# Fewer weight decodings beside the first eight head pairs, the rms weight folded into the decoding, and a new order for the first pair

## The chip, the cores and the metric

The kernel runs on one core of a Trainium2 chip. The metric is the time of one execution on the device, in microseconds (us), as a median of several runs. A measurement of this kernel tells differences of about 0.5% (6.7 us) from no change.

## The reference

```python
# q, k, v: 8 batches x 8 heads x 576 tokens x 64, w_phi: 64 x 128
proj = x @ w_phi;  proj = proj - max|proj| (per token)
phi(x) = [exp(proj), exp(-proj)]                 # 256 features
kv = sum_s phi(k) v;  z = sum_s phi(k)
attn = (phi(q) kv) / (phi(q) z + 1e-6)           # -> x: 4608 tokens x 512
xn = x / sqrt(mean(x*x) + 1e-6) * rms_g
g = xn @ w_gate;  val = xn @ w_val               # 512 x 1536 each
out = (silu(g) * val) @ w_out                    # 1536 x 512
```

The three weights and `rms_g` of the second half are stored as 64-bit floats (`rms_g` as read by the kernel is 32-bit); the kernel turns each weight into 32-bit floats itself, and calls that decoding. Products that have to be exact are computed from a high and a low part of each operand, as three matmuls (high x high, high x low, low x high).

## The kernel before, in words

The program has three stages: the attention (0 to about 525 us), the products with `w_gate` and `w_val` (to about 1065 us), and the product with `w_out`. The change touches the attention stage.

**Rounds.** The 64 heads are taken as 32 pairs. The loop at line 500 runs over rounds `i`. In round i, `front(i)` transposes and projects pair i, `mid(i-1)` takes exponentials and accumulates kv for the pair before, `back(i-2)` forms numerator and denominator, `last(i-3)` divides and stores the result to `xs` in DRAM. The inverse of the denominator goes through DRAM by four DMAs one after the other: `dd` out, `dr` in, reciprocal, `di` out, `rc` in as a broadcast (lines 419 to 428); line 442 then waits for `rc`.

**front.** `trans` transposes k (`kt`), q (`qt`) or the rests (`rb`, the 64 tokens of k and q that don't fill a block of 128) and splits the result into `th` and `tl` (line 61 on VectorE). `proj` multiplies by the split `w_phi` (`wh`, `wl`, lines 311 to 313), takes the largest magnitude (`mx`, line 315) and subtracts it (`yk`, `yq`, `yr`, line 318). There are two PSUM buffers `pp` and three `sm`.

**Decoding.** Each round takes one job from `decs` (`dq += 1`, line 510): one fetch of 128 x 384 weights (`raw`), two ScalarE instructions (lines 48, 49), three VectorE instructions on bits (50 to 52), two GpSimd products (54), and one VectorE sum (55). The first eight jobs belong to `wf1`, the part of the weights that stays in SBUF: there line 235 multiplies by `g`, the rms weight, and `_split` makes a high and a low part (lines 60, 61; `fg`, `fv`). The other 24 are written to DRAM (`wgs`, `wvs`).

**Fills.** From about 191 us the first products with `wf1` (line 474, `fp<-xo`) run beside the attention. A block of 288 tokens is fetched (`x<-xs`, line 142), split into `xo` (lines 60, 61), and gives six units. When the attention ends the remaining units run alone. `x0`, the first block of the second stage, is fetched in round 27 and its squares (lines 147, 150) are placed from round 29.

**Order.** The code gives pieces positions within a round (`_spread`, `_merge`), and a scheduler then fixes the order of instructions on each engine. On each engine, and in each DMA queue, instructions start in that order: one that waits holds all behind it. `late()` ties an instruction behind those already issued on its engine.

Of the kernel before, what the change touches and what calls it, by code (L numbers as in the profile page):

```python
# [8 lines left out]
F32 = mybir.dt.float32  # L9
F32R = mybir.dt.float32r  # L10
I32 = mybir.dt.int32
U32 = mybir.dt.uint32
AF = mybir.ActivationFunctionType
ALU = mybir.AluOpType
# [23 lines left out]
    return raw  # L38


def _decode(nc, pool, raw, n):
    if raw.dtype == F32:
        return raw
    low, high = raw[:, :, 0], raw[:, :, 1]
    p = pool.tile([128, n], I32, name="wp", bufs=2)
    a = pool.tile([128, n], F32, name="wa", bufs=2)
    u, lf = a.bitcast(I32), low.bitcast(F32)
    nc.scalar.mul(a, high.bitcast(F32), REBASE)
    nc.scalar.mul(lf, low.bitcast(U32), 2.0 ** -52)
    nc.vector.tensor_scalar(p, u, 3, None, ALU.logical_shift_left)  # L50
    nc.vector.scalar_tensor_tensor(p, u, -0x80000000, p, ALU.bitwise_and, ALU.bitwise_or)
    nc.vector.tensor_scalar(u, p, -0x00800000, None, ALU.bitwise_and)
    for h in (slice(0, n // 2), slice(n // 2, n)):
        nc.gpsimd.tensor_tensor(a[:, h], lf[:, h], a[:, h], ALU.mult)  # L54
    nc.vector.tensor_tensor(a, p.bitcast(F32), a, ALU.add)
    return a


def _split(nc, hi, lo, x, hi_copy=None, lo_eng=None):
    (hi_copy or nc.scalar.copy)(hi, x)  # L60
    (lo_eng or nc.vector).tensor_tensor(lo, x, hi.bitcast(F32), ALU.subtract)  # L61
# [21 lines left out]
def kernel(ctx: ExitStack, tc: tile.TileContext, q, k, v, w_phi,  # L83
                         w_gate, w_val, w_out, rms_g, out):
    nc = tc.nc
# [3 lines left out]
    NC, NJ = DM // 128, DF // 128  # L89
# [23 lines left out]
    gl = ctx.enter_context(tc.tile_pool(name="gl", bufs=1))  # L113
    eps = gl.tile([128, 1], F32, name="eps")
    nc.vector.memset(eps, 1e-6)
    g = gl.tile([128, NC], F32, name="g")

# [69 lines left out]
    dec = a_ctx.enter_context(tc.tile_pool(name="a_dec", bufs=1))  # L189
# [23 lines left out]

    vms = [const.tile([128, 2, T0, D + 1], F32, name=f"vm{i}") for i in range(3)]
    vrs = [const.tile([128, 2, D + 1], F32, name=f"vr{i}") for i in range(3)]
    for vm, vr in zip(vms, vrs):
        nc.gpsimd.memset(vm, 1.0)
        nc.gpsimd.memset(vr, 1.0)
        nc.gpsimd.memset(vr[64:128, 0], 0.0)
        nc.gpsimd.memset(vr[0:64, 1], 0.0)  # L220
# [8 lines left out]
    def decode_jobs():  # L229
        jobs, late_ = [], []  # L230
        n = J1 * 128
        for wi, src in enumerate((w_gate, w_val)):
            for c in range(NC):
                def fill_w(w, wi=wi, c=c):
                    nc.vector.tensor_scalar(w, w, g[:, c:c + 1], None, ALU.mult)
                    _split(nc, wf1[wi][0][:, c], wf1[wi][1][:, c], w)
                jobs.append((src[c * 128:(c + 1) * 128, 0:n], n, fill_w))

        def keep(jobs, src, dst, r0, c0, n):
            at = slice(r0, r0 + 128), slice(c0, c0 + n)  # L240
            jobs.append((src[at], n, lambda w: nc.sync.dma_start(out=dst[at], in_=w)))

        for c0 in range(n, DF, 384):
            for src, dst in ((w_gate, wgs), (w_val, wvs)):
                for c in range(NC):
                    keep(jobs, src, dst, c * 128, c0, 384)
        for j in range(NJ):
            for c0 in range(0, DM, CH):
                keep(late_, w_out, wos, j * 128, c0, CH)
        return jobs, late_  # L250

    def decode_pieces(jobs, dec):
        raws = {}

        def piece(i):
            if i == 0:
                raws[0] = _fetch(nc, dec, *jobs[0][:2])
            raw = raws.pop(i)
            if i + 1 < len(jobs):
                raws[i + 1] = _fetch(nc, dec, *jobs[i + 1][:2])  # L260
            with late():
                jobs[i][2](_decode(nc, dec, raw, jobs[i][1]))
        return [lambda i=i: piece(i) for i in range(len(jobs))]

    st = {}
# [20 lines left out]
    def front(pr):  # L286
        d = st[pr]
        f = {n: d[n].rearrange("p h t d -> p (h t d)") for n in ("kt", "qt")}
        us = {n: [f[n + "t"][:, i * 128:(i + 1) * 128] for i in range(4)] for n in "kq"}
        us["r"] = [d["rb"].rearrange("p a d -> p (a d)")]  # L290
        d["y"] = {}
        hl = {}

        def trans(n):
            m = len(us[n]) * 128
            tp = ps_s.tile([128, 512], F32, name="sm")
            for j, u in enumerate(us[n]):
                nc.tensor.transpose(out=tp[:, j * 128:(j + 1) * 128], in_=u, identity=ident)
            th = wk.tile([128, 512], F32R, name="th")
            tl = wk.tile([128, 512], F32R, name="tl")  # L300
            _split(nc, th[:, 0:m], tl[:, 0:m], tp[:, 0:m])
            hl[n] = (th, tl)

        def proj(n, u0):
            th, tl = hl[n]
            m = min(2, len(us[n]) - u0)
            pp = ps_p.tile([128, 4, F], F32, name="pp")
            for j in range(m):
                o = pp[:, 2 * j:2 * j + 2].rearrange("p a f -> p (a f)")
                cs = slice((u0 + j) * 128, (u0 + j + 1) * 128)  # L310
                nc.tensor.matmul(o, th[:, cs], wh, start=True, stop=False)  # L311
                nc.tensor.matmul(o, th[:, cs], wl, start=False, stop=False)
                nc.tensor.matmul(o, tl[:, cs], wh, start=False, stop=True)  # L313
            mx = wk.tile([128, 4], F32, name="mx")
            nc.vector.tensor_reduce(mx[:, 0:2 * m], pp[:, 0:2 * m], axis=AX.X, op=ALU.max,  # L315
                                    apply_absolute_value=True)
            y = wk.tile([128, 4 if n != "r" else 2, F], F32, name="y" + n, bufs=3 if n != "r" else 2)
            nc.vector.tensor_tensor(y[:, 0:2 * m], pp[:, 0:2 * m],  # L318
                                    mx[:, 0:2 * m].unsqueeze(2).broadcast_to([128, 2 * m, F]), ALU.subtract)
            d["y"][n, u0 // 2] = y  # L320

        return [lambda: trans("r" if pr else "k"), lambda: trans("k" if pr else "r"),
                lambda: proj("r", 0), lambda: proj("k", 0), lambda: trans("q"), lambda: proj("k", 2), lambda: proj("q", 0), lambda: proj("q", 2)]

# [161 lines left out]
    dq = quota = 0.0  # L486
# [8 lines left out]
            units.extend(fill(*here.pop(0)))  # L495

    load(0)
    nc.sync.dma_start(out=g, in_=rms_g.rearrange("(c p) -> p c", p=128))
    load(1)
    for i in range(PR + 3):  # L500
        streams = []
        if i < PR:
            streams.append(_spread(front(i), -0.2, 0.7))
# [3 lines left out]
            streams.append(back(i - 2))  # L507
        if 0 <= i - 3 < PR:
            streams.append(last(i - 3))
        dq += 1  # L510
        dl, decs = decs[:int(dq)], decs[int(dq):]
        dq -= int(dq)
        streams.append(dl)
# [30 lines left out]
    dec = g_ctx.enter_context(tc.tile_pool(name="m_dec", bufs=1, reuse_waits="tile"))  # L544
# [261 lines left out]
```

## Time and profile before

| | us |
|---|---|
| median of 3 runs | 1340.66 (1338.13 to 1345.27) |
| the profiled execution's own time | 1340.64 |
| its span, first to last instruction | 1338.7 |
| TensorE busy | 1288.7 (96%) |
| VectorE busy | 884.2 (66%) |
| ScalarE busy | 711.7 (53%) |
| GpSimd busy | 606.9 (45%) |

The busy shares are means over stages with different limits, and a matmul's duration overlaps its neighbours', so the number of matmuls in a stretch says more of TensorE than its busy time. PE is TensorE, DVE VectorE, ACT ScalarE, POOL GpSimd, SP the queue from which most DMAs are issued.

### The profile page before, as it was taken

The numbers are of one execution on the slowest core, as the hardware profiler recorded it, in microseconds if no ns is written. First come the engines' busy times: TensorE is split into PE (matmuls) and PEld (weight loads), VectorE is DVE, ScalarE is ACT, GpSimd is POOL, SyncE is SP. The second block draws the span as 40 slices with busy tenths as digits, with TensorE's granted clock in tenths as the row PEclk, the third lists the DMA queues.
The fourth block names the chain that finished last, engine by engine and source line by source line (L and its number), as shares of the span: only waits on it lengthen the run. The fifth ranks groups of instructions, "written<-read, shape, count | busy, mean of one in ns | idle before, by whom it ended". The sixth has DMA issues, their size and how long they took to land.

```text
span 1338.7 us, 25484 instructions
## 1 busy us (share of the span) xinstructions
PE 1288.7 (96%) x9396; PEld 1274.0 (95%) x9396; DVE 884.2 (66%) x1301; ACT 711.7 (53%) x1510; POOL 606.9 (45%) x568
## 2 busy tenths in 40 slices
PE   7989999999999897998999999999999999999998
PEld 6889899999999897998999999999999999999998
DVE  7899888787778772114566656655434498877774
ACT  5988877778778782344444344433333334434332
POOL 4766565555556570000232223233221078787675
PEclk9999999999999898999999999999999999999999
DMA  6456566665555434446454454554433533454451
GB/s 164 124 144 156 163 161 161 173 167 169 154 165 159 120 102 149 141 145 192 149 168 148 159 166 138 166 164 143 132 114 109 183 111 126 149 167 127 138 161 65
DMA packets 204524, 197.21 MB, mean 147 GB/s; under 512 B 69553, under 2 KB 186417, under 8 KB 204401
## 3 DMA queue, kind: packets, MB, share of 16 engines
q1 hardware_dynamic: 194896, 190.88, 47.9%
q10 hardware_dynamic: 9504, 4.72, 1.3%
q8 instruction: 74, 1.21, 0.4%
q14 instruction: 50, 0.40, 0.1%
HBM read 126.04 MB, written 69.50 MB: 146 GB/s over the span
## 4 chain that ended last, share of the span: by engine, by line
PE 55%; DVE 3%; DMA 2%; ACT 1%; issue 1%; POOL 0%; ACTq 0%; SPq 0%; DVEq 0%
PE fp L588 16%; PE gp L588 16%; PE fp L474 6%; PE gd L742 5%; PE gz L742 5%; PE gy L742 5%; PE fp L742 2%; DMA wc<-wvs 1%; DMA wc<-wgs 1%; DVE xo L61 0%; DVE a12l L61 0%; DMA rc<-di 0%; DVE a11l L61 0%; DVE ri L160 0%; POOL s2l L61 0%
## 5 line engine op out<-in xcount | busy, mean ns | idle before, releaser
L380 POOL TENSOR_TENSOR ql<-eq,qh 128x256 fp32r<-128x256 f32 x256 | 218.0, 882 | 66.2 <-issue 39.1
L588 PE MATMUL fp<-xb,wg 128*128 128x384 f32 x864 | 163.4, 337 | 4.4 <-ACT wg L60 4.3
L588 PE MATMUL gp<-xb,wv 128*128 128x384 f32 x864 | 161.5, 334 | 0.0
L588 PEld LDWEIGHTS fp<-xb,wg 128*128 128x128 f32 x864 | 152.1, 189 | 5.0 <-ACT wg L60 4.5
L588 PEld LDWEIGHTS gp<-xb,wv 128*128 128x128 f32 x864 | 150.9, 188 | 0.0
L573 DVE TENSOR_TENSOR h<-sl,gp 128x384 f32<-128x384 f32 x108 | 59.5, 551 | 127.6 <-PE gp L588 59.5
L571 ACT ACTIVATE sl<-fp 128x384 f32<-128x384 f32 x108 | 52.7, 489 | 165.8 <-PE fp L588 144.6
L54 POOL TENSOR_TENSOR wa<-raw,wa 128x192 f32<-128x192 f32 (+1 forms) x112 | 67.5, 623 | 159.6 <-ACT sl L571 51.7
L351 PE MATMUL acc<-vm,ek 128*128 128x65 f32 x1024 | 131.7, 271 | 0.0
L351 PEld LDWEIGHTS acc<-vm,ek 128*128 128x128 f32 x1024 | 128.1, 195 | 0.2 <-ACT ek L338 0.2
L315 DVE TENSOR_REDUCE mx<-pp 128x4 f32<-128x512 f32 (+1 forms) x160 | 100.4, 631 | 39.8 <-PE pp L313 38.2
L61 POOL TENSOR_TENSOR xb<-x,xb 128x1536 fp32r<-128x1536 f32 x12 | 42.8, 3563 | 151.7 <-ACT xb L60 151.7
L151 POOL TENSOR_TENSOR ss<-ss,sq 128x384 f32<-128x384 f32 x36 | 38.6, 1071 | 153.9 <-ACT sq L150 153.9
L474 PE MATMUL fp<-xo,fg 128*128 128x288 f32 x576 | 96.5, 305 | 9.1 <-DVE xo L61 9.1
L376 ACT ACTIVATE qh<-sm 128x512 fp32r<-128x512 f32 (+1 forms) x192 | 96.9, 505 | 0.0
L474 PEld LDWEIGHTS fp<-xo,fg 128*128 128x128 f32 x576 | 82.4, 191 | 12.4 <-DVE xo L61 11.4
L474 PE MATMUL fp<-xo,fv 128*128 128x288 f32 x576 | 92.5, 299 | 0.0
L311 PE MATMUL pp<-wh,th 128*128 128x256 f32 x288 | 88.2, 308 | 4.3 <-DVE yr L318 3.6
L61 POOL TENSOR_TENSOR s2l<-st,s2h 128x768 fp32r<-128x768 f32 x18 | 43.6, 2420 | 97.4 <-DVE h L573 44.2
L375 ACT ACTIVATE eq<-sm 128x512 f32<-128x512 f32 x128 | 78.1, 610 | 12.8 <-PE sm L364 11.7
L313 PE MATMUL pp<-wh,tl 128*128 128x256 f32 x288 | 82.3, 295 | 2.2 <-DVE tl L61 2.2
L588 PE MATMUL fp<-xb,fg 128*128 128x384 f32 x432 | 81.1, 335 | 0.6 <-ACT sl L571 0.5
(198 smaller groups left out, 3794.2 us busy)
## 6 DMA issues: line engine op xcount, KB each, us to landing
hs<-h SPq DMA_DIRECT2D x144, 192.0 KB
ht<-hs SPq DMA_DIRECT2D x18, 1536.0 KB
gvs<-fo SPq DMA_DIRECT2D x96, 144.0 KB
gvr<-gvs SPq DMA_DIRECT2D x36, 384.0 KB
rc<-di SPq DMA_DIRECT2D x32, 288.0 KB
x<-xs SPq DMA_DIRECT2D x16, 576.0 KB
x<-xs SPq DMA_DIRECT2D x12, 768.0 KB
kt<-in_k_dram SPq DMA_DIRECT2D x32, 256.0 KB
```

Of the source, the lines that this page charges most:

```text
L54: nc.gpsimd.tensor_tensor(a[:, h], lf[:, h], a[:, h], ALU.mult)
L61: (lo_eng or nc.vector).tensor_tensor(lo, x, hi.bitcast(F32), ALU.subtract)
L311: nc.tensor.matmul(o, th[:, cs], wh, start=True, stop=False)
L313: nc.tensor.matmul(o, tl[:, cs], wh, start=False, stop=True)
L315: nc.vector.tensor_reduce(mx[:, 0:2 * m], pp[:, 0:2 * m], axis=AX.X, op=ALU.max, apply_absolute_value=True)
L351: nc.tensor.matmul(acc[:, sg, h], e[h][:, sg, j], vm[:, h, j], start=False, stop=(h == 1 and j == T0 - 1))
L375: nc.scalar.activation(ei[:, sg], yi, AF.Exp, scale=1.0 - 2.0 * sg)
L376: nc.scalar.activation(hi[:, sg], yi, AF.Exp, scale=1.0 - 2.0 * sg)
L380: nc.gpsimd.tensor_tensor(lo[:, sg, cs], ei[:, sg, cs], hi[:, sg, cs].bitcast(F32), ALU.subtract)
L474: nc.tensor.matmul(fp[:, 0:TF], w, xx[x][:, c], start=(i == 0), stop=(i == 3 * NC - 1))
L588: nc.tensor.matmul(gp[:, 0:T], w, e[:, c], start=(i == 0), stop=(i == 3 * NC - 1))
L742: nc.tensor.matmul(place[n], a[:, kp], w[:, o], start=(first and kp == 0 and i == 0), stop=(kp == KP - 1 and i == 2), skip_group_check=True)
```

## The change

Four edits. The decoding takes half a job a round in rounds 0 to 7 and 1.2 jobs from round 8 on (32 jobs end in round 31 as before). For the `wf1` jobs the multiplication by `g` is no longer an instruction of its own: the high part is multiplied in the sum (line 55 becomes a scalar_tensor_tensor), the low part by a scale `g * 2^-52` per partition in place of the constant in line 49; one small instruction computes that scale, `g52`. The first pair's rests come after k and q. The load of `g` is issued behind the loads of the second pair, and the GpSimd memsets of `vm` come before those of `vr`.

```diff
-def _decode(nc, pool, raw, n):
+def _decode(nc, pool, raw, n, scale=None):
...
-    nc.scalar.mul(lf, low.bitcast(U32), 2.0 ** -52)
+    nc.scalar.mul(lf, low.bitcast(U32), scale[1] if scale else 2.0 ** -52)
...
-    nc.vector.tensor_tensor(a, p.bitcast(F32), a, ALU.add)
+    if scale:
+        nc.vector.scalar_tensor_tensor(a, p.bitcast(F32), scale[0], a, ALU.mult, ALU.add)
+    else:
+        nc.vector.tensor_tensor(a, p.bitcast(F32), a, ALU.add)
...
-    for vm, vr in zip(vms, vrs):
+    for vm in vms:
         nc.gpsimd.memset(vm, 1.0)
+    for vr in vrs:
         nc.gpsimd.memset(vr, 1.0)
...
-                    nc.vector.tensor_scalar(w, w, g[:, c:c + 1], None, ALU.mult)
                     _split(nc, wf1[wi][0][:, c], wf1[wi][1][:, c], w)
-                jobs.append((src[c * 128:(c + 1) * 128, 0:n], n, fill_w))
+                jobs.append((src[c * 128:(c + 1) * 128, 0:n], n, fill_w, (g[:, c:c + 1], g52[:, c:c + 1])))
...
+        if pr == 0:
+            return [lambda: trans("k"), lambda: proj("k", 0), lambda: trans("q"), lambda: proj("k", 2),
+                    lambda: trans("r"), lambda: proj("r", 0), lambda: proj("q", 0), lambda: proj("q", 2)]
...
     load(0)
+    load(1)
     nc.sync.dma_start(out=g, in_=rms_g.rearrange("(c p) -> p c", p=128))
-    load(1)
+    nc.vector.tensor_scalar(g52, g, 2.0 ** -52, None, ALU.mult)
...
-        dq += 1
+
+        dq += 0.5 if i < 8 else 1.2
```

The edits also change what the scheduler does far from them. Three places follow; the line numbers are those of each kernel's own file.

TensorE, the first instructions of the program; `sm<-ident,kt` is the transpose of k, `rb` the rests, `pp` the projections. Before:

```order
L298 MATMUL sm_191<-ident_129,kt_168 128x128 x4
L298 MATMUL sm_200<-ident_129,rb_172 128x128
L298 MATMUL sm_225<-ident_129,qt_169 128x128 x4
L311 MATMUL pp_206<-wh_134,th_202 128x256
L312 MATMUL pp_206<-wl_135,th_202 128x256
L311 MATMUL pp_214<-wh_134,th_196 128x256
L312 MATMUL pp_214<-wl_135,th_196 128x256
L313 MATMUL pp_214<-wh_134,tl_197 128x256
L311 MATMUL pp_214<-wh_134,th_196 128x256
```

and in the changed kernel:

```order
L306 MATMUL sm_193<-ident_130,kt_169 128x128 x4
L306 MATMUL sm_213<-ident_130,qt_170 128x128 x4
L319 MATMUL pp_202<-wh_135,th_198 128x256
L319 MATMUL pp_222<-wh_135,th_198 128x256
L320 MATMUL pp_202<-wl_136,th_198 128x256
L320 MATMUL pp_222<-wl_136,th_198 128x256
L306 MATMUL sm_233<-ident_130,rb_173 128x128
L321 MATMUL pp_202<-wh_135,tl_199 128x256
L319 MATMUL pp_202<-wh_135,th_198 128x256
L320 MATMUL pp_202<-wl_136,th_198 128x256
```

The transposes of q and four projection matmuls of k now stand ahead of the transposes of the rests.

VectorE, the end of the attention; `nd<-nd,rc` are the divisions of the last two pairs (lines 442 and 443 before), `xo` the low parts of a block for the fills, each in two halves. Before:

```order
L425 RECIPROCAL dr_7642<-dr_7642 128x9
L61 TENSOR_TENSOR xo_7752<-x_7134,xo_7752 128x576 x2
L442 TENSOR_TENSOR nd_7640<-nd_7640,rc_7739 64x576
L443 TENSOR_TENSOR nd_7640<-nd_7641,rc_7739 64x576
L425 RECIPROCAL dr_7793<-dr_7793 128x9
L61 TENSOR_TENSOR xo_7923<-x_7136,xo_7923 128x576
L442 TENSOR_TENSOR nd_7791<-nd_7791,rc_7837 64x576
L443 TENSOR_TENSOR nd_7791<-nd_7792,rc_7837 64x576
L61 TENSOR_TENSOR xo_7923<-x_7136,xo_7923 128x576
```

and in the changed kernel:

```order
L68 TENSOR_TENSOR xo_7746<-x_7128,xo_7746 128x576 x2
L436 RECIPROCAL dr_7636<-dr_7636 128x9
L453 TENSOR_TENSOR nd_7634<-nd_7634,rc_7733 64x576
L454 TENSOR_TENSOR nd_7634<-nd_7635,rc_7733 64x576
L436 RECIPROCAL dr_7787<-dr_7787 128x9
L68 TENSOR_TENSOR xo_7917<-x_7130,xo_7917 128x576 x2
L453 TENSOR_TENSOR nd_7785<-nd_7785,rc_7831 64x576
L454 TENSOR_TENSOR nd_7785<-nd_7786,rc_7831 64x576
L68 TENSOR_TENSOR xo_8020<-x_7783,xo_8020 128x576 x2
```

Both halves of the second block (`xo_7917`) now stand ahead of the last division, which before stood between the two halves (`xo_7923`); and the first block's (`xo_7746`) stand ahead of the reciprocal that they followed.

The SP queue around the load of `x0` (`x<-xs`, 128x4x384, line 142 before). Before:

```order
L446 DMA xs_57<-nd_6352 128x576
L241 DMA wvs_61<-wa_6729 128x384
L426 DMA di_6610<-dr_6608 128x9
L273 DMA kt_7138<-in_k_dram 128x2x256
L281 DMA vr1_146<-in_v_dram 64x64
L142 DMA x_6589<-xs_57 128x4x384
L428 DMA rc_6793<-di_6610 64x1152
L419 DMA dd_6872<-nd_6869 1x576
L273 DMA qt_7139<-in_q_dram 128x2x256
```

and in the changed kernel:

```order
L457 DMA xs_57<-nd_6333 128x576
L437 DMA di_6591<-dr_6589 128x9
L281 DMA kt_7132<-in_k_dram 128x2x256
L288 DMA vm1_144<-in_v_dram 128x4x64
L439 DMA rc_6787<-di_6591 64x1152
L289 DMA vr1_147<-in_v_dram 64x64
L281 DMA qt_7133<-in_q_dram 128x2x256
L150 DMA x_6570<-xs_57 128x4x384
```

The load of `x0` now stands behind the broadcast load `rc` and the load of `qt`; before it stood ahead of both.

## Rows read from the trace of the kernel before

**Rows 1.** The page's busy time by engine, whole span.

```profile
PE 1288.7 (96%) x9396; PEld 1274.0 (95%) x9396; DVE 884.2 (66%) x1301; ACT 711.7 (53%) x1510; POOL 606.9 (45%) x568
```

**Rows 2.** Stretches: length, busy us (records) of PE, PEld, DVE, ACT, POOL; PEclk, DMA, GB/s.

```profile
22.61:119.57 96.96, 89.34 (x736) 86.67 (x737) 88.35 (x162) 81.85 (x203) 64.17 (x79) 1.00 0.55 144
119.57:199.70 80.13, 76.78 (x623) 73.75 (x622) 68.92 (x126) 66.27 (x165) 50.66 (x64) 1.00 0.59 157
199.70:425.60 225.90, 224.49 (x1860) 223.47 (x1860) 178.85 (x306) 173.88 (x434) 125.38 (x153) 1.00 0.61 168
119.57:131.06 11.49, 11.49 (x97) 11.02 (x96) 11.32 (x22) 10.74 (x27) 8.33 (x10) 1.00 0.57 137
448.00:458.00 10.00, 9.10 (x42) 9.10 (x43) 4.44 (x7) 5.35 (x15) 6.46 (x8) 0.50 0.33 97
525.00:530.00 5.00, 4.59 (x20) 4.59 (x21) 0.35 (x1) 0.80 (x2) 0.00 (x0) 0.52 0.81 233
```

**Rows 3.** VectorE by form, 0 to 150 us: count | busy us, mean ns | idle before.

```profile
L55 DVE TENSOR_TENSOR wa<-wp,wa 128x384 f32<-128x384 f32 x10 | 8.2, 816 | 0.2 <-POOL wa L54 0.2
L51 DVE SCALAR_TENSOR_TENSOR wp<-wa,wp 128x384 int32<-128x384 int32 x10 | 6.9, 688 | 0.1
L235 DVE TENSOR_SCALAR wa<-wa,g 128x384 f32<-128x384 f32 x8 | 5.3, 661 | 0.0
L50 DVE TENSOR_SCALAR wp<-wa 128x384 int32<-128x384 int32 x10 | 4.1, 410 | 2.0 <-ACT wa L48 2.0
L52 DVE TENSOR_SCALAR wa<-wp 128x384 int32<-128x384 int32 x10 | 4.0, 402 | 0.0
L61 DVE TENSOR_TENSOR fv<-wa,fv 128x384 fp32r<-128x384 f32 x4 | 2.5, 632 | 1.3 <-ACT fv L60 1.3
```

**Rows 4.** ScalarE by form, 0 to 150 us.

```profile
L49 ACT ACTIVATE raw<-raw 128x384 f32<-128x384 uint32 x10 | 5.6, 555 | 0.0
L60 ACT CAST fv<-wa 128x384 fp32r<-128x384 f32 x4 | 2.1, 513 | 4.2 <-DVE wa L235 4.2
```

**Rows 5.** Instructions that read tile g, whole span: ns min/median/max, first and last start.

```profile
L162 DVE SCALAR_TENSOR_TENSOR x<-x,g,ri x48: 605/614/1092, 482.8 to 1018.6; 128x384 f32<-128x384 f32 x48
```

**Rows 6.** Timeline, all engines, 0 to 13 us: start, duration, instruction, [idle before <-releaser].

```profile
5.26 0.41 ACT L60 CAST wh<-wa 128x256 fp32r<-128x256 f32 x1
...
6.01 0.42 DVE L61 TENSOR_TENSOR wl<-wa,wh 128x256 fp32r<-128x256 f32 x1
...
6.88 0.59 SPq L498 DMA_DIRECT2D g<-in_moe_rms_g_dram  x1
...
7.26 0.45 PE L298 MATMUL sm<-ident,rb 128*128 128x128 f32 x1 [2.51 <-DMA rb<-in_q_dram]
...
8.21 0.56 PE L311 MATMUL pp<-wh,th 128*128 128x256 f32 x1
...
10.52 1.02 DVE L315 TENSOR_REDUCE mx<-pp 128x2 f32<-128x256 f32 x2 [2.19 <-PE pp L313]
...
12.17 0.62 SPq L281 DMA_DIRECT2D vr<-in_v_dram  x1
...
12.61 0.36 PE L311 MATMUL pp<-wh,th 128*128 128x256 f32 x1 [2.13 <-DVE yr L318]
```

**Rows 7.** Timeline of SP, of ScalarE and of TensorE around x0, 439 to 450 us.

```profile
439.86 0.53 SPq L142 DMA_DIRECT2D x<-xs  x1
441.89 0.48 SPq L428 DMA_DIRECT2D rc<-di  x1
...
447.25 0.52 ACT L147 ACTIVATE ss<-x 128x384 f32<-128x384 f32 x1 [2.85 <-DMA x<-xs]
...
448.90 1.11 PE L298 MATMUL sm<-ident,kt 128*128 128x128 f32 x4 [2.78 <-ACT qh L376]
```

**Rows 8.** Timeline of VectorE, then of TensorE, at the end of the attention.

```profile
517.26 0.74 DVE L61 TENSOR_TENSOR xo<-x,xo 128x576 fp32r<-128x576 f32 x1
523.03 0.75 DVE L442 TENSOR_TENSOR nd<-nd,rc 64x576 f32<-64x576 f32 x1 [5.03 <-DMA rc<-di]
523.81 0.75 DVE L443 TENSOR_TENSOR nd<-nd,rc 64x576 f32<-64x576 f32 x1
524.59 0.76 DVE L61 TENSOR_TENSOR xo<-x,xo 128x576 fp32r<-128x576 f32 x1
...
525.41 1.57 PE L474 MATMUL fp<-xo,fg 128*128 128x288 f32 x5 [5.36 <-DVE xo L61]
```

More of the change, by code (lines that the diff above doesn't have):

```diff
@@ L38, in _fetch @@
     return raw
-def _decode(nc, pool, raw, n):
+def _decode(nc, pool, raw, n, scale=None):
     if raw.dtype == F32:
+        if scale:
+            nc.vector.tensor_scalar(raw, raw, scale[0], None, ALU.mult)
         return raw
@@ L54, in _decode @@
         nc.gpsimd.tensor_tensor(a[:, h], lf[:, h], a[:, h], ALU.mult)
-    nc.vector.tensor_tensor(a, p.bitcast(F32), a, ALU.add)
+    if scale:
+        nc.vector.scalar_tensor_tensor(a, p.bitcast(F32), scale[0], a, ALU.mult, ALU.add)
+    else:
+        nc.vector.tensor_tensor(a, p.bitcast(F32), a, ALU.add)
     return a
@@ L116 @@
     g = gl.tile([128, NC], F32, name="g")
+    g52 = gl.tile([128, NC], F32, name="g52")
     x_ctx = ExitStack()
@@ L261, in piece @@
             with late():
-                jobs[i][2](_decode(nc, dec, raw, jobs[i][1]))
+                jobs[i][2](_decode(nc, dec, raw, jobs[i][1], *jobs[i][3:]))
         return [lambda i=i: piece(i) for i in range(len(jobs))]
```

## The prediction

> **What bounds the kernel now.** I read the busy times first: TensorE is busy for 1288.7 of 1338.7 us [rows 1], so all that a change of order can win lies in TensorE's gaps and in stretches where its matmuls start slowly. Then I cut the attention into stretches, because its limit changes there, and compared the number of TensorE records per us. The fastest short stretch gives 97 records in 11.49 us, 8.44 per us; from 199.7 to 425.6 us, with the fills beside it, TensorE keeps 8.23 per us, 97.5% of that, and is busy for 224.49 of 225.9 us [rows 2]. There TensorE is the bound, and what VectorE does is hidden. From 22.61 to 119.57 us (from the second pair's `yr` to the ninth's) VectorE is busy for 88.35 of 96.96 us, its instructions almost back to back, and TensorE keeps only 7.59 per us, 90% [rows 2]. There VectorE sets the pace. From there to 199.7 us it is 7.77 per us, 92%, with VectorE at 86%: nobody is the bound alone [rows 2]. The timelines then show three single losses: at the start, where TensorE waits 2.51 us for the rests and 2.13 us for VectorE [rows 6]; at 446 us, where ScalarE waits for `x0` [rows 7]; and at 520 us, where one division holds half a split [rows 8].
>
> **The start.** Before, the first projection starts at 8.21 us, behind the rests, which landed at 7.26; `wh` is made from 5.26 to 5.67 and `wl` until 6.43 [rows 6]. In the new order the projections of k need only k, `wh` and `wl`, so they can start at about 6.1, 2.1 us sooner, and VectorE's first maximum, at 10.52, moves with them. The maximum of k is also no longer behind that of the rests. I take -2.5 us; the bounds are 0 (the other loads are just as late) and -4.6, both waits of TensorE. The load of `g` moves behind eight issues, from 6.88 to about 12.2 us, where the second pair's last one stands [rows 6]; `g52` waits for it and VectorE's queue behind it. It comes after the maxima and differences of the first pair, near 14.5 us by the order, so I expect at most 1 us here, inside those bounds.
>
> **Rounds 1 to 8.** In the stretch from 22.61 to 119.57 us the order shows 24 VectorE instructions fewer: three whole decodings, 3 x (0.410 + 0.688 + 0.402 + 0.816) = 6.95 us; seven multiplications by `g`, 7 x 0.661 = 4.63; four splits, 4 x 0.632 = 2.53 [rows 3]; the last, of kv, only crosses the boundary. VectorE falls from 88.35 to about 74.2 us. ScalarE falls by three pairs of conversions and four casts, 3 x 2 x 0.555 + 4 x 0.513 = 5.4 [rows 4], to about 76.5. TensorE's work stays: 736 records at 8.44 per us are 87.2 us [rows 2], and that is now the last to come. So at most 9.8 us can go. At the 92% of the next stretch it would be 94.8 us, a gain of 2.2; at the 97.5% of the filled stretch 89.4, a gain of 7.6. VectorE's share would be 82%, between those two stretches (86% and 79%), so I take the middle, -5, and the ends 0 and -9.8.
>
> The new sum with a scalar (scalar_tensor_tensor, 128x384) has no row of its own: the same operation, with `g` as its scalar, takes 0.614 us at line 162 [rows 5], the old sum 0.816, the same operation on integers 0.688 [rows 3]. I take it as unchanged; the ends are -0.2 and +0.2 each, 1.6 us over eight, all on VectorE.
>
> Here the trace and a rule part. The multiplication by `g` took 0.661 us and integer operations of the same shape 0.41 [rows 3]. The Trainium skill, page "VectorE: DVE Perf Modes", section "The perf-mode tier table (the rule you actually need)", gives a 32-bit tensor_scalar in SBUF two elements a cycle and tensor_tensor one, so by it the multiplication should cost about half a sum, by estimate 0.41 us. By that the seven removed would be worth 2.9 us and not 4.63, VectorE would stay 1.8 us higher, and the gain would still be within the ends above.
>
> **Rounds 8 to 14.** What left the first rounds comes here: the order shows seven decodings for six, four of them with splits, and one kv split more. VectorE gets 2.32 + 4 x 0.632 + 0.42 = 5.3 us [rows 3], 68.92 becomes 74.2 of 80.13, 93%, near the 91% of the stretch before it. If TensorE's rate falls from 92% to that stretch's 90%, 623 records take 82.0 us. I take +2; the ends are 0 and +5.3, VectorE's whole addition.
>
> **The filled rounds, 199.7 to 425.6 us.** Two decodings more, 4.6 us on VectorE, which is busy for 178.85 of 225.9 [rows 2]. TensorE hides them: 0, at the most +4.6 if the cover were gone.
>
> **x0.** ScalarE reached the squares of `x0` and waited 2.85 us for its load; TensorE stood still for 2.78 us behind it [rows 7] and then ran at a granted clock of 0.50 (1.2 GHz) from 448 to 458 us, 42 records where 84 fit: another 5 us [rows 2]. In the new SP order the load stands behind `rc` and `qt`; before, `rc` was issued 2 us after it [rows 7]. So it lands about 2 us later, while ScalarE comes to the squares less than 1 us later (four short exponentials of the rests now stand ahead). I take +2. The ends are -7.8 (no wait, no slow clock) and +5.
>
> **The end of the attention.** Before, the second half of the split `xo` waited in VectorE's queue behind lines 442 and 443, and line 442 waited 5.03 us for `rc`; so TensorE stood for 5.36 us [rows 8] and then ran at a mean clock of 0.52, 20 records in 5 us, about 2 us lost [rows 2]. In the new order both halves come first, and nothing that they need is late: the first half ran at 517.26. So 7.4 us go. What is late next are the stores of `fo`: SP still waits for that division before it stores `xs`, and three buffers hold the fills' results meanwhile; I allow 0.9 us for it. -6.5; the ends are 0 and -7.4.
>
> **Sum.** -2.5 - 5 + 2 + 0 + 2 - 6.5 = -10. The profiled execution took 1340.64 us, 1.94 more than its span and within 0.1 of the median of the runs shown. So I forecast 1330.6 us, 0.7% faster.
>
> **The rivals.** *The early rounds are a chain, not VectorE's load.* Then their gain is that of the 92% rate, -2.2, and the start gives -1; the sum is -5.7, 1334.9 us. For it: the stretch after 119.57 us lost 8% with VectorE at 86%. Against it: VectorE there has waits, and before 119.57 hardly any. 20%.
>
> *The end keeps its loss.* Another wait, of ScalarE's queue or a load, stands where the division stood: -10 + 6.5 = -3.5, 1337.1 us. Against it: TensorE's wait ended 0.06 us after the half split did [rows 8]. 12%.
>
> *The wait for x0 goes.* If ScalarE comes later than I think, TensorE's pause is short and its clock stays at 2.4 GHz: instead of +2 it is -7.8, so -19.8, 1320.8 us. For it: a shift of 3 us in 440 does it. Against it: the load's new place. 12%.
>
> *Slower: VectorE waits for the divisions' loads in the early rounds.* With rounds of about 13 us instead of 14, the four DMAs of the inverse have less time, and line 442, in order, stands for `rc` as it did for 5.03 us at 518 [rows 8]. Each such stop long enough to lower TensorE's clock costs what x0 did, 2.8 + 5 = 7.8 us [rows 2, 7]; from two of them on the kernel is slower than before, -10 + 15.6 = +5.6, 1346.2 us. Against it: before, such waits came only at the end, when VectorE had nothing else, and a round leaves the chain several us of room. 8%. The Trainium skill has the rule in "TensorE: Matmul & The Clock Gate", section "HAM oscillation — how this bites in real kernels": bursts of matmuls that are parted by waits for data run each time at the lower rate. The trace agrees at 448 us (0.50) [rows 2].
>
> That the scheduler doesn't do what the numbers say is excluded by the order: four decodings stand before the ninth pair's `yr`, where eight stood.
>
> **How the numbers follow.** The forecast has 48%, with 1325 to 1335 as its own range; the rivals have 20, 12, 12 and 8%. About 0.5%, 6.7 us, is what a measurement can tell from no change: faster means under 1334. That holds for nearly all of the forecast (44), the rival without x0's wait (12) and three in ten of the chain (6): 62%. Slower by as much is the last rival and a little of others: 9%. The rest, 29%, is the same. The range from 1318 to 1341 takes in both better and worse rivals, and leaves out the slower one.
>
> **What would show it.** VectorE busy for about 74 us between the second and the ninth `yr`, 24 instructions fewer, and that stretch at about 92 us; the first projection near 6.1 us; a wait of ScalarE at the squares of `x0` of 3 to 5 us; no division between the halves of `xo` and no pause of TensorE of 5 us near 510. I am wrong if TensorE's rate in the early rounds stays at 7.6 per us though VectorE has gaps, if a new stretch at the lower clock appears, or if the fills stop at the same point for another reason.

## The result, and the profile after

The changed kernel took 1348.66 us (median of 8 runs, 1344.48 to 1353.65) against 1341.86 for the kernel before on the same chip: a ratio of 1.0063, with a 95% interval from 1.0047 to 1.0078. It is slower, where I had forecast 0.7% faster. Measured once more on another chip the ratio was 1.0091 (1.0067 to 1.0116). Single executions of one kernel lie up to 15 us apart (1331.35 to 1346.44 us in one version below), so the medians decide, and the profiles give the places.

The profiled execution spans 1347.2 us, 8.5 more than before. The first view is the changed kernel cut into the stretches of [rows 2], with the two stages behind the attention added (columns as there).

```profile
19.64:120.02 100.38, 91.43 (x724) 88.11 (x724) 78.55 (x137) 79.82 (x197) 58.93 (x75) 0.97 0.50 132
120.02:203.53 83.51, 78.36 (x651) 76.63 (x650) 74.31 (x134) 70.56 (x175) 51.65 (x64) 1.00 0.56 151
203.53:429.16 225.63, 224.82 (x1862) 223.54 (x1861) 184.90 (x317) 175.91 (x437) 129.79 (x159) 1.00 0.61 172
429.16:612.61 183.45, 166.91 (x1207) 161.59 (x1204) 77.16 (x120) 96.55 (x227) 57.20 (x64) 0.95 0.44 137
612.61:1069.27 456.66, 455.45 (x2614) 454.58 (x2615) 254.33 (x386) 180.94 (x319) 103.78 (x99) 1.00 0.48 152
1069.27:1342.30 273.03, 270.62 (x2269) 269.76 (x2268) 206.38 (x177) 105.55 (x143) 200.34 (x90) 1.00 0.41 127
```

The same three last stretches of the kernel before:

```profile
425.61:611.08 185.47, 165.63 (x1208) 160.73 (x1206) 74.92 (x116) 96.09 (x225) 54.75 (x62) 0.95 0.43 132
611.08:1067.60 456.52, 455.80 (x2614) 454.58 (x2615) 253.84 (x386) 180.82 (x319) 104.81 (x99) 1.00 0.48 152
1067.60:1333.80 266.20, 263.33 (x2269) 262.33 (x2268) 204.75 (x177) 101.29 (x143) 200.22 (x90) 1.00 0.42 130
```

Line by line against [rows 2], the difference of 8.5 us is: start -2.97 (the second `yr` at 19.64 for 22.61), rounds 1 to 8 +3.42, rounds 8 to 14 +3.38, filled rounds -0.28, `x0` and the end of the attention together -2.02, second stage +0.14, third stage +6.83. The third stage, none of whose instructions the change touches and which I had not looked at, holds the largest term: the same 2269 records at the same granted clock of 1.00 with TensorE never idle for long, 273.0 us instead of 266.2.

**The third stage.** Twenty microseconds out of its middle, before and after:

```profile
1200.00:1220.00 20.00, 20.00 (x175) 20.00 (x175) 13.97 (x12) 7.14 (x10) 15.51 (x8) 1.00 0.55 175
```

```profile
1200.00:1220.00 20.00, 20.00 (x170) 20.00 (x170) 15.19 (x14) 7.78 (x10) 16.72 (x8) 1.00 0.58 182
```

TensorE is busy all the time in both, but starts 175 matmuls before and 170 after. By the start times, a product of 18 matmuls takes 2.08 us before and 2.14 after, in every group. Nothing waits; the matmuls start further apart. What the change does do here is to move data, so it does not touch the attention stage alone, as I wrote ahead of the prediction: the new tile `g52` takes 32 bytes per partition near the bottom of the on-chip memory, and all tiles that are stacked above it move up by 32 bytes. That holds for the third stage's stationary operands (`a11h` from byte 105248 to 105280), while four of the six pairs of weights `wh`, `wl` are stacked from the other end and stay where they were. A product takes three matmuls with each pair of weights. With the four pairs that stayed, the three took 1, 16, 18 and 12 ns more than before (medians, by the start times); with the two that moved along, 10 and 3 more.

**The early rounds.** Two stretches now run at a lower clock, and before there were none. First the clock in the changed kernel, then in the same windows before:

```profile
80.00:85.00 5.00, 2.92 (x14) 2.39 (x15) 4.75 (x9) 3.84 (x10) 4.83 (x6) 0.86 0.54 162
85.00:90.00 5.00, 5.00 (x36) 5.00 (x36) 1.95 (x4) 2.06 (x7) 1.10 (x2) 0.80 0.25 64
110.00:115.00 5.00, 2.15 (x13) 1.71 (x12) 4.56 (x8) 5.00 (x12) 3.69 (x4) 0.93 0.77 151
115.00:120.00 5.00, 5.00 (x34) 5.00 (x34) 3.23 (x5) 0.76 (x2) 2.39 (x3) 0.73 0.41 127
```

```profile
80.00:85.00 5.00, 3.98 (x31) 3.74 (x31) 4.96 (x9) 4.24 (x10) 5.00 (x7) 1.00 0.38 96
85.00:90.00 5.00, 5.00 (x45) 5.00 (x44) 4.94 (x10) 3.55 (x11) 3.84 (x5) 1.00 0.68 195
110.00:115.00 5.00, 4.88 (x40) 4.72 (x41) 4.96 (x9) 5.00 (x12) 3.99 (x5) 1.00 0.61 127
115.00:120.00 5.00, 5.00 (x45) 4.91 (x43) 4.37 (x10) 1.76 (x5) 2.57 (x3) 1.00 0.44 147
```

VectorE's timeline and TensorE's waits at the first of the two, in the changed kernel:

```profile
79.48 1.07 DVE L60 SCALAR_TENSOR_TENSOR wa<-wp,g,wa 128x384 f32<-128x384 f32 x1
80.47 0.68 DVE L326 TENSOR_TENSOR yq<-pp,mx 128x512 f32<-128x512 f32 x1
81.07 0.74 DVE L453 TENSOR_TENSOR nd<-nd,rc 64x576 f32<-64x576 f32 x1
81.84 1.18 DVE L454 TENSOR_TENSOR nd<-nd,rc 64x576 f32<-64x576 f32 x1
83.05 0.21 DVE L436 RECIPROCAL dr<-dr 128x9 f32<-128x9 f32 x1
83.18 0.37 DVE L68 TENSOR_TENSOR kv0l<-acc,kv0h 128x260 fp32r<-128x260 f32 x1
```

```profile
79.06 0.63 PE L375 MATMUL sm<-ident,yq 128*128 128x128 f32 x4 [0.56 <-DVE yq L326]
81.52 0.39 PE L319 MATMUL pp<-wh,th 128*128 128x256 f32 x1 [0.50 <-ACT th L67]
83.60 0.61 PE L426 MATMUL fp<-qh,kv0l 128*128 128x288 f32 x1 [1.58 <-DVE kv0l L68]
```

The low half of the kv split, `kv0l`, stands behind both divisions (lines 453 and 454) and the reciprocal, which take 2 us together. TensorE's next product needs it. Pauses of 0.56, 0.50 and 1.58 us stand within 5 us, the last of them for `kv0l`; in the two windows of 5 us 14 and 36 matmuls start, where before it was 31 and 45. The fifth kv split does this at 83 us, the seventh at 114 us (2.35 us). In the kernel before the split stood ahead of the divisions in that same round:

```profile
82.05 0.42 DVE L61 TENSOR_TENSOR kv0l<-acc,kv0h 128x260 fp32r<-128x260 f32 x1
82.38 0.28 DVE L61 TENSOR_TENSOR tl<-sm,th 128x128 fp32r<-128x128 f32 x1
82.58 0.68 DVE L318 TENSOR_TENSOR yq<-pp,mx 128x512 f32<-128x512 f32 x1
83.18 0.74 DVE L442 TENSOR_TENSOR nd<-nd,rc 64x576 f32<-64x576 f32 x1
83.95 1.04 DVE L443 TENSOR_TENSOR nd<-nd,rc 64x576 f32<-64x576 f32 x1
```

The place behind the divisions is not enough by itself. In the kernel before, the sixth split stood there too, and TensorE paused 1.24 us for it, 3.4 us after another pause of 1.23 us, and the clock stayed at 1.00:

```profile
97.96 0.21 DVE L425 RECIPROCAL dr<-dr 128x9 f32<-128x9 f32 x1
98.09 0.37 DVE L61 TENSOR_TENSOR kv1l<-acc,kv1h 128x260 fp32r<-128x260 f32 x1
...
98.52 0.40 PE L415 MATMUL fp<-qh,kv1l 128*128 128x288 f32 x1 [1.24 <-DVE kv1l L61]
```

**x0 and the end**, to compare with [rows 7, 8]. SP now issues `rc` first and `x0` 2.2 us after it; ScalarE, later too, waits 1.24 us; TensorE stops for 3.33 us:

```profile
443.36 0.49 SPq L439 DMA_DIRECT2D rc<-di  x1
445.57 0.37 SPq L150 DMA_DIRECT2D x<-xs  x1
...
451.61 0.52 ACT L155 ACTIVATE ss<-x 128x384 f32<-128x384 f32 x1 [1.24 <-DMA x<-xs]
...
454.55 0.40 PE L426 MATMUL sm<-qh,kv0h 128*128 128x288 f32 x1 [3.33 <-ACT qh L387]
```

At the end (ScalarE's rows, then TensorE's), the pause of 5.36 us is gone, but the buffers `fo` wait for their stores:

```profile
520.16 0.40 ACT L488 COPY fo<-fp 128x288 f32<-128x288 f32 x1 [2.38 <-DMA gvs<-fo]
520.45 1.25 ACT L67 CAST xo<-x 128x576 fp32r<-128x576 f32 x2
525.19 0.40 ACT L488 COPY fo<-fp 128x288 f32<-128x288 f32 x1 [3.49 <-DMA gvs<-fo]
...
521.18 0.40 PE L485 MATMUL fp<-xo,fg 128*128 128x288 f32 x1 [0.68 <-ACT xo L67]
522.53 1.06 PE L485 MATMUL fp<-xo,fg 128*128 128x288 f32 x6 [0.95 <-DVE xo L68]
525.64 1.57 PE L485 MATMUL fp<-xo,fv 128*128 128x288 f32 x5 [2.06 <-ACT fo L488]
```

Three shorter pauses, 3.7 us together, stand where one of 5.4 stood, and the clock falls behind them as it did before: 18 matmuls start from 525 to 530 us at 0.50, before it was 20 at 0.52. At 506 us TensorE also waits 1.95 us for a kv split behind two divisions, with a clock of 0.68 from 505 to 510 us; before, a wait of 2.20 us for a kv split at 503 us left the clock at 1.00.

### The profile page after: what moved, and what is told of

It is laid out like the page before. It is cut to its first block, busy times and chain, and to the rows that moved or that the text cites. A ratio compares the mean times of both kernels' runs of the same rounds, so it can differ in the third digit from the quotient of the medians.

```text
span 1347.2 us, 25468 instructions
## 1 busy us (share of the span) xinstructions
PE 1301.9 (97%) x9396; PEld 1287.0 (96%) x9396; DVE 888.1 (66%) x1294; ACT 716.8 (53%) x1510; POOL 605.6 (45%) x568
## 4 chain that ended last, share of the span: by engine, by line
PE 79%; DVE 9%; DMA 5%; ACT 4%; issue 1%; POOL 0%; SPq 0%; ACTq 0%; DVEq 0%; POOLq 0%
PE fp L601 15%; PE gp L601 15%; PE fp L485 9%; PE acc L362 6%; PE gd L755 5%; PE gz L755 5%; PE gy L755 5%; PE sm L426 3%; PE fp L755 3%; PE fp L426 2%; PE pp L319 2%; PE pp L321 2%; PE pp L320 2%; PE sm L375 2%; PE sm L306 2%; DMA wc<-wvs 2%
## 5 line engine op out<-in xcount | busy, mean ns | idle before, releaser
L391 POOL TENSOR_TENSOR ql<-eq,qh 128x256 fp32r<-128x256 f32 x256 | 221.2, 894 | 100.2 <-issue 49.0
L58 POOL TENSOR_TENSOR wa<-raw,wa 128x192 f32<-128x192 f32 (+1 forms) x112 | 63.9, 591 | 140.3 <-ACT sl L584 52.4
L485 PEld LDWEIGHTS fp<-xo,fv 128*128 128x128 f32 x576 | 82.3, 191 | 2.3 <-ACT fo L488 2.3
L321 PE MATMUL pp<-wh,tl 128*128 128x256 f32 x288 | 83.4, 300 | 0.0
```

Of the source, the lines that this page charges most:

```text
L391: nc.gpsimd.tensor_tensor(lo[:, sg, cs], ei[:, sg, cs], hi[:, sg, cs].bitcast(F32), ALU.subtract)
L485: nc.tensor.matmul(fp[:, 0:TF], w, xx[x][:, c], start=(i == 0), stop=(i == 3 * NC - 1))
```

## The experiments

**The addresses.** Making the tile of `g` longer moves all that is stacked above it, and the order on every engine stays the same, instruction for instruction.

```diff
 # changed kernel: 240 + 16 bytes, so all is 256 bytes above its place in the kernel before
-    g = gl.tile([128, NC], F32, name="g")
+    g = gl.tile([128, 60], F32, name="g")[:, 0:NC]
```

> The changed kernel with the tile of g made 240 bytes long per partition, so that every tile behind it in the left half of the on-chip memory has the address of the kernel before plus 256 bytes instead of plus 32; the order on every engine is that of the changed kernel. Theory A (the third stage is slower because g52 moved its operands by 32 bytes against the weights on the right side): the 18 products of a third-stage group take 2.08 us again and not 2.14, the third stage 271 us and not 278, the median 1341.5 us (1340 to 1343), the attention stays as in the changed kernel. Theory B (the third stage is slower because of what the other engines do beside it, in another phase): nothing changes, 1348.7 us.

Measured: 1341.77 us against 1335.78 (1.0044, 1.0028 to 1.0061). Third stage 265.9 us; the marks of the attention are those of the changed kernel (ninth `yr` at 119.67, second stage at 612.2). So the rest of the change costs 0.44% here, 5.9 us. The first measurement, less the 0.5% of the addresses, leaves 0.13% for it, as the two profiles do; the two intervals just meet, at 0.28%.

```diff
 # kernel before: 48 bytes, two slots of 32 instead of one
-    g = gl.tile([128, NC], F32, name="g")
+    g = gl.tile([128, 12], F32, name="g")[:, 0:NC]
```

> The kernel before with the tile of g made 48 bytes long per partition, so that the tiles behind it move by 32 bytes as g52 moved them; the order on every engine is that of the kernel before. Theory A (addresses): the third stage takes 278 us, the median is 1348.8 us (1347.5 to 1350.5), slower by 0.5%, though not one instruction has changed. Theory B (other engines beside it): 271 us, 1341.9 us, no change.

Measured: 1344.65 us (1.0047, 1.0029 to 1.0065). Third stage 272.7 us, with no instruction changed. The same 20 us in these two runs, the changed kernel put back first, then the kernel before with the longer tile:

```profile
1200.00:1220.00 20.00, 20.00 (x175) 20.00 (x174) 14.80 (x14) 7.47 (x11) 15.16 (x8) 1.00 0.63 190
```

```profile
1200.00:1220.00 20.00, 20.00 (x170) 20.00 (x170) 16.18 (x15) 8.23 (x11) 15.91 (x9) 1.00 0.39 122
```

175 and 170 records change sides with the addresses and not with the order. Theory A holds both ways, at 7.1 and 6.5 us.

> The kernel before with the stationary operands of the second and third stage laid out in steps of 32 bytes: from pair to pair (a11, a12, s2, s3, s1) and from weight block to weight block (j) the address moves by 32 more. The order is unchanged. Theory A: the spacing of the matmuls differs from one operand to the next, about 0.1156 us at one step and 0.1190 at another in the third stage, and perhaps other values in the second stage, where it has been 0.1733 in both kernels. Theory B: one spacing for all operands of a stage.

```diff
-    h, l = (opools.get(n, xof).tile(part, F32R, name=n + i) for i in "hl")
+    h, l = (opools.get(n, xof).tile([128, KP * 128 + (8 if i == "l" and n in ("a11", "a12", "s2", "s3") else 0)], F32R, name=n + i)[:, 0:KP * 128].rearrange("p (k n) -> p k n", n=128) for i in "hl")
```

The edit lets the low tile of `a11`, `a12`, `s2` and `s3`, and (in a second line, not shown) the last weight tile of each `j` in the second stage, end 32 bytes later. Measured (one execution, third stage 269.5 us): 18 matmuls take 2.08 us with `a11`, `s4` and `a22`, which did not move, 2.13 with `a12` (32 bytes further), 2.15 with `s2` (64), 2.14 with `s3` (96), 2.12 to 2.13 with `s1` (128). The weights stood still, so moving the stationary operand is enough. In the second stage 12 matmuls took 2.08 to 2.12 us and nowhere less than before. Which places are good, and why, these runs do not settle: in the changed kernel the matmuls whose two operands moved together became slower too (the 10 and 3 ns above), so the distance between the two is not shown to be all of it.

**The parts of the change, one at a time,** at addresses with which 18 matmuls of the third stage take 2.08 us. The new rate alone:

```diff
-        dq += 1
+        dq += 0.5 if i < 8 else 1.2
```

> The kernel before with the new decoding rate alone (0.5 jobs a round for eight rounds, then 1.2); no tile moves. My forecast gave the rounds 1 to 8 a gain of about 4 us from fewer decodings and 2 us back later. Theory C (what the lighter VectorE gives in the early rounds is lost again in pauses of TensorE of 1 to 2.4 us that lower its clock, since a late kv split now leaves TensorE without other work): the ninth pair's yr comes at 119 to 121 us as in the kernel before, with one or more stretches below full clock before 120 us; total 1341 to 1345 us. Theory D (the clock falls come from the fold or the first pair's order and not from the rate): no stretch below full clock before 120 us, the ninth yr at 114 to 117 us, total 1336 to 1340 us.

1347.23 us (1.0080, 1.0055 to 1.0105). The ninth `yr` came at 126.3, worse than theory C had it; four pauses of 1.2 to 1.6 us for `kv0l`, at 57, 87, 118 and 180 us, each with a clock below 0.8 behind it.

The first pair's order alone (the edits of the change with `pr == 0`, `load(1)` and the memsets):

> The kernel before with the first pair's order alone (k and q ahead of the rests, the load of g behind the second pair's loads, the memsets). By my forecast the second yr comes 2.5 us sooner (22.6 to about 20), the ninth too, and the kernel is 2.5 us, 0.2%, faster: theory H, the gain at the start is kept. Theory I, it is lost within the eight rounds that VectorE bounds: the ninth yr stays within 1 us of 119.6, and the time is the same.

1344.45 us against 1339.02 (1.0045, 1.0026 to 1.0064): the second `yr` at 19.7, the ninth at 121.0, the fifteenth at 209.9 instead of 199.7. Theory I, and worse: the 3 us are lost, and by the fifteenth `yr` 10 more. TensorE waits 2.21 us for `kv0l` at 112 us, with a clock of 0.56, 0.50 and 0.58 from 110 to 125 us.

The fold alone (`scale` in the decoding, `g52`):

> The kernel before with the multiplication by g folded into the decoding alone (its tile does not move the third stage's operands). Eight instructions of 0.66 us leave VectorE. Theory J (VectorE bounds the rounds 1 to 8): the ninth yr comes 3 to 5 us sooner, 115 to 117 us, the kernel is 0.2 to 0.4% faster. Theory K (the rounds are a chain through several engines): the ninth yr moves by less than 1.5 us and the time is the same within 0.15%.

1347.07 us (1.0058, 1.0037 to 1.0079); the ninth `yr` at 122.9, the fifteenth at 209.8. Eight multiplications less on VectorE, and slower: neither theory. Pauses of 1.80 and 1.98 us for `kv0l` at 87 and 115 us; the clock falls behind the second alone.

Fold and first pair without the rate:

```diff
-        dq += 0.5 if i < 8 else 1.2
+        dq += 1
```

> The changed kernel with the third stage's addresses put back and the decoding rate put back to one job a round: what is left of the change is the folded weight and the first pair's order. Theory C (the rate is what costs): no stretch below full clock before 200 us, the ninth yr at 114 to 117 us (3 us from the start and a part of the 4.6 us of multiplications), 0.2 to 0.5% faster than the kernel before. Theory G (any new order of VectorE, also from the fold or the first pair, puts kv behind the divisions): the clock still falls before 120 us and the time is the same as before or slower.

1337.65 us (1.0000, 0.9977 to 1.0022): the ninth `yr` at 121.1 behind a clock of 0.58 and 0.50 from 95 to 105 us, the fifteenth at 198.4. That is theory G: another kv split behind the divisions, at 97 us, and the time of the kernel before. Theory C was too hopeful; the rate is not all of it. The parts don't add up: alone each costs 0.45 to 0.8%, two together nothing. Each makes the scheduler write another order, and as far as these runs show the order sets the time.

**The order of one instruction.** The divisions, and with them the reciprocal and the loads behind it, are moved behind the kv split, in the changed kernel with put-back addresses (the longer tile of `g`):

```diff
-        return [(0.65, fin)]
+        return [(1.1, fin)]
...
-                (0.5, lambda: num(1, 1)), (0.79, inv)]
+                (0.5, lambda: num(1, 1)), (1.2, inv)]
```

> The changed kernel with the third stage's addresses put back (as in the run with the long tile of g), and the two divisions and the inverse moved later in a round (0.65 to 1.1, 0.79 to 1.2), so that on VectorE each split of kv stands ahead of the two divisions. Theory C (with the new rate the third, fifth and seventh kv split stand behind both divisions and the reciprocal, about 2 us; TensorE waits for them right after two shorter pauses and its clock falls to half): the pauses of 1.6 and 2.4 us for kv0l and both stretches below full clock before 120 us are gone, the ninth pair's yr comes at 112 to 116 us instead of 119.7, the median is 4 to 8 us under that of the same kernel without this edit, 1334 to 1338 us where the kernel before takes 1336. Theory F (TensorE pauses because VectorE's work is bunched in every second round, wherever kv stands): the pauses move to another instruction, the clock still falls, the ninth yr stays at 118 to 120 us and the time within 2 us of 1341.8.

1347.42 us (1.0066, 1.0040 to 1.0092). The ninth `yr` came at 114.4, without a clock below 1.00 till then, as theory C said; but the later rounds gave it all back (second stage at 621.2). So only the early pairs, first those with `pr < 6` (then 5, then three single ones):

```diff
+        return [(1.1 if pr < 6 else 0.65, fin)]                 # the last run: pr in (0, 2, 4)
...
+                (0.5, lambda: num(1, 1)), (1.2 if pr < 6 else 0.79, inv)]    # and pr in (1, 3, 5)
```

> The changed kernel with the third stage's addresses put back and the late divisions in the first rounds alone (pairs 1 to 6; from the seventh on they stand where the change has them). With late divisions throughout, the ninth pair's yr came at 114.4 us and not at 119.7, but the rounds after it gave all of it back. Theory C: the gain of the early rounds is kept when the later rounds have their old places: ninth yr at 114 to 116 us, the fifteenth at 198 to 200 instead of 203, no stretch below full clock before 130 us, the median 4 to 6 us under that of the same kernel without the edit, equal to the kernel before or up to 0.3% faster. Theory L (what is won early is lost in the rounds 9 to 14, since their order is as good as fixed by another engine): the fifteenth yr comes at 202 to 204 us all the same.

1340.79 us against 1336.82 (1.0026, 1.0009 to 1.0043): the ninth `yr` at 113.7, the fifteenth at 199.6, both about where theory C had them. The time is not: it is 0.18% under the put-back version's ratio of 1.0044, about 2 us, where 4 to 6 were expected. One stop is left, shown by VectorE and TensorE in that run's timeline, and by the clock behind it:

```profile
113.66 0.41 DVE L326 TENSOR_TENSOR yr<-pp,mx 128x256 f32<-128x256 f32 x1
118.22 0.75 DVE L453 TENSOR_TENSOR nd<-nd,rc 64x576 f32<-64x576 f32 x1 [4.15 <-DMA rc<-di]
118.99 1.19 DVE L454 TENSOR_TENSOR nd<-nd,rc 64x576 f32<-64x576 f32 x1
120.20 0.69 DVE L68 TENSOR_TENSOR tl<-sm,th 128x512 fp32r<-128x512 f32 x1
...
120.95 0.48 PE L306 MATMUL sm<-ident,rb 128*128 128x128 f32 x1 [4.27 <-DVE tl L68]
```

```profile
120.00:125.00 5.00, 3.83 (x18) 3.43 (x19) 4.65 (x9) 2.95 (x6) 2.15 (x3) 0.66 0.36 111
```

This is the stop that my slower rival described: a division that waits for `rc`, TensorE behind it, a clock of 0.66. The same edit with the old rate:

> The same late divisions in the first rounds, with the old decoding rate: fold, first pair's order and third stage's addresses as in the run with the rate put back, where one stretch (95 to 110 us) ran below full clock behind a wait of 1.4 us for a kv split, and the ninth yr came at 121.1 us. Theory C: that stretch goes, the ninth yr comes at 115 to 118 us, the stage of the gate and value products starts 3 to 6 us sooner than 605.9, and the kernel is 0.2 to 0.5% faster than the kernel before. Theory M (any edit of these places changes the order of the later rounds too, which costs more): same as before or slower, with rounds of 14.4 us and more between the ninth and the fifteenth yr.

1344.69 us (1.0065, 1.0042 to 1.0088): theory M. The ninth `yr` came at 118.1, and the rounds to the fifteenth took 89.0 us. The same stop stands in them: a division waits 3.79 us for `rc` until 122.9 us, and TensorE 5.54 us behind it. The changed kernel once more:

> The changed kernel itself once more, on the chip of the two runs beside it, to compare it with the version with put-back addresses. If the addresses cost 6.8 us and nothing else differs, it is 0.5% slower than that version: 1.0095 of the kernel before by the ratio of 1.0044 measured there, against 1.0063 measured for it first.

1349.12 us (1.0091, 1.0067 to 1.0116), 0.47% above the put-back version's 1.0044; 6.8 us of addresses are 0.5%.

The stop at 118 us goes if the sixth pair keeps its old places (`pr < 5`), so that its chain of loads starts sooner:

> As the run with late divisions in the early rounds, but for pairs 1 to 5 only, so that the sixth pair's division and inverse stand at their old places: the chain of four loads behind that inverse starts 0.4 of a round sooner. Theory C (single waits in VectorE's order cost the time): the wait of 4.15 us for rc at 118 us and TensorE's stop of 4.3 us are gone, the ninth yr stays at 113 to 116 us, the fifteenth comes at 192 to 197 us instead of 199.6, and the median is 3 to 7 us lower than that run's: 0.1 to 0.4% faster than the kernel before. Theory N (the rounds 9 to 14 take 14 us each whenever the early ones are short, as something in them is fixed): the fifteenth yr stays at 199 to 203 us and the kernel is the same as before or slower.

1329.51 us against 1338.35: 0.9928 (0.9908 to 0.9949), the one version whose whole interval lies more than 0.5% below the kernel before, and a larger gain than the 0.1 to 0.4% that I expected. No pause of TensorE reaches 1 us from 15 to 205 us, and the clock is 1.00 throughout. Its four stretches of the attention:

```profile
19.37:113.52 94.15, 90.12 (x748) 87.50 (x748) 77.90 (x138) 79.53 (x199) 59.56 (x75) 1.00 0.54 141
113.52:195.01 81.49, 78.27 (x639) 75.65 (x638) 72.13 (x134) 67.86 (x172) 49.43 (x64) 1.00 0.58 154
195.01:419.93 224.92, 223.33 (x1851) 222.07 (x1850) 185.00 (x317) 176.07 (x438) 129.56 (x158) 1.00 0.60 173
419.93:600.67 180.74, 164.87 (x1207) 160.07 (x1204) 73.89 (x120) 97.11 (x227) 54.77 (x64) 0.96 0.45 139
```

And with only the three divisions late that had held a kv split:

> As the run before it, but only the divisions of the first, third and fifth pair are late, the three behind which the third, fifth and seventh kv split stood. Theory C: the same as with five late ones, within 2 us: no pause over 1.2 us for kv0l before 120 us, ninth yr at 113 to 117 us, 0 to 0.4% faster than the kernel before. Theory N: fifteenth yr at 199 us or later, and same or slower.

1331.25 us (0.9948, 0.9928 to 0.9967): the ninth `yr` at 114.1, the fifteenth at 194.6. Theory C, by a little more than the 0.4% it allowed. By the two ratios, 1.0044 and 0.9948, the late places of three pairs' divisions are worth nearly 1%; 5.5 us of it stand at the ninth `yr`, the rest in later rounds, whose order changed with them.

## Why the prediction was wrong

**The sum lacked a term.** I had priced each instruction and each wait of the attention and put the other stages at nothing without a reason. The new tile `g52` was there in the change, with its one instruction costed (at most 1 us; it ran at 16.95 us and waited for nothing); its 32 bytes were not. They cost 6.5 to 7.1 us, in an order that is the same instruction for instruction.

**Rounds 1 to 8: -5 forecast, +3.4 measured.** The load fell, by 9.8 us of the 14.1 worked out: 25 instructions fewer on VectorE (24 forecast), 78.55 us busy (74.2 forecast; the scaled sum took 0.92 us and not 0.82, the splits of `fg` 0.83). The step that failed is the next one, that a VectorE with gaps gives its time to TensorE: TensorE's rate fell to 7.2 matmuls per us (724 in 100.38 us) from 7.6. The gaps came where the next product had to wait for a kv split: the scheduler had put it behind two divisions, in every second round. From 80 to 90 and from 110 to 120 us, where the clock fell, 64 matmuls fewer start than before; at 8.44 per us that is 7.6 us, an estimate, of the 8.4 between forecast and result. I named this as what would prove me wrong (a new stretch at the lower clock), but gave the only rival with it, a wait for `rc`, 8%, and looked for waits of VectorE on loads, not for what stands ahead of a split in its queue. The order was there to be read. With the split ahead of the divisions the stretch took 94.15 us for 748 matmuls. That is 7.9 per us, near the 8.0 that 736 in 92 us would be, so the rate was about right and its condition was missed; in time it is a gain of 2.8 us and not 5, for 12 more matmuls fell inside the stretch. (VectorE's share at 92 us would have been 81%, not 82%; nothing hung on it. Of the two prices for the multiplication by `g`, the lower, 0.41 us, is the fastest of the eight, and the median was 0.61.)

**The rival of a chain** (20%) had the early rounds gain 2.2 us; they lost. **The slower rival** had the wrong instruction, though its mechanism, stops of TensorE that are each followed by a lower clock, is what happened, with 0.86 and 0.80 behind the pauses at 83 us. That its 1346.2 us lie near the measured time is luck: the two stops cost 3.1 and 4.5 us by the estimate above, not 7.8 each, and the 32 bytes and the end of the attention made up the rest. On the lower rate behind a pause the trace agrees with the section "HAM oscillation — how this bites in real kernels" of the Trainium skill's page "TensorE: Matmul & The Clock Gate"; the pauses here, 1.58 us at most at 83 us, are shorter than the waits of the page's example.

**Start: -2.5 forecast, -2.97 measured.** The first projection started at 5.94 us (6.1 forecast). The gain is real and was kept until the first stop: the sixth `yr` came 3.9 us sooner than before (70.66 for 74.57), the seventh 1.0 later (88.44 for 87.44).

**Rounds 8 to 14: +2 forecast, +3.4 measured**, inside its ends of 0 and +5.3, but by the order more than by the load. In the orders whose ninth to thirteenth kv split stand beside the next round's `yr`, the stretch took 77.3 (rate put back), 80.1 (before), 80.4 and 81.5 us (the two last runs); in all orders with most of these splits among the `yq`, 83.4 to 89.0. That goes together in eleven kernels; it was not changed alone.

**Filled rounds:** 0 forecast, -0.28. **x0 and the end:** +2 and -6.5 forecast, -2.0 together; cut at the 31st `yr` (459.72 before, 462.48 after) it is -0.8 and -1.2. ScalarE's wait at `x0` was 1.24 us (3 to 5 forecast) and yet TensorE stopped longer than before; the lower clock behind it was shorter (0.56 and 0.75 from 455 to 465 us, before 0.79, 0.50 and 0.69 from 445 to 460).

At the end no division stands between the halves of `xo`, as forecast, but the step that nothing they need is late failed: ScalarE makes the high half at 520.45, behind a copy that waits 2.38 us for a store. What I had allowed 0.9 us for, the stores of `fo`, took 2.06, and the clock fell all the same. So **the rival that the end keeps its loss** (12%), by another wait of ScalarE's queue, is what came, all but 1.2 us; no run changed the stores to test it.

In the best version `x0` and the end gain 4.7 us, near the 4.5 of the two terms, and its attention ends 10.4 us sooner than before (600.67 for 611.08), where my whole sum was -10. That the two agree is in part luck: from the start to the end of the attention its terms are -3.2, -2.8, +1.4, -1.0 and -4.7, for -2.5, -5, +2, 0 and -4.5 forecast, in an order found by trial.

## What to carry to other kernels

Look at what a change does to memory as well as to time: a small tile that is allocated early moves every tile stacked above it, and where matmuls come back to back, the place of an operand can change their spacing (here 2.08 or 2.14 us for 18). Test it by making the tile longer without touching the order. Where a scheduler writes the order, a part of a change is not worth what its instructions take: read in the new order what stands ahead of each small instruction that TensorE waits for, and how close together such waits fall; if a gain is missing, move what stands ahead before the change is given up.

## What was not expected of the hardware

- Matmuls of 256 columns in an uninterrupted stream started every 115.6 ns (2.08 us for 18) or every 118.9 ns (2.14), by 32 bytes in the address of their stationary operand. The second stage, where both operands moved together, kept its time (456.52 and 456.66 us); in the third stage matmuls whose operands moved together did not (10 and 3 ns for three).
- No single long stop is needed for a lower clock: pauses of 0.56, 0.50 and 1.58 us were followed by 0.86 and 0.80, while pauses of 1.23 and 1.24 us at 95 and 98 us of the kernel before were not, nor were 1.66 and 1.80 us at 83 and 87 us with the fold alone. The length of a pause does not settle it, and what does is not shown here.
